# Attention into two MLPs on one core: two head pairs go over to split multiplication, and two weight units are prepared later

## The chip, the cores and the metric

The kernel runs on one core of a Trainium2 chip. The metric is the device time in microseconds (us) of one execution. The core has a matrix engine (TensorE, PE in the profile; its weight loads are PEld), a vector engine (VectorE, DVE), a scalar engine (ScalarE, ACT), GpSimd (POOL), and SyncE (SP), which issues this kernel's DMAs.

## The reference

```python
# q, k, v: 4 batches, 12 heads, 448 tokens, head size 64
scores = cap * tanh((q @ k.T / 8) / cap)
attn   = exp(scores - max(scores)); attn = attn / (sum(attn) + 1e-9)
x = (attn @ v)            # put together as 1792 tokens x 768
x = relu(x @ w_in)**2  @ w_out      # first MLP,  768 -> 2048 -> 768
x = relu(x @ w_in2)**2 @ w_out2     # second MLP, 768 -> 2048 -> 768
```

The weights arrive as 64-bit floats; all else is float32.

## The kernel before, in words

**Stages.** Attention works on pairs of heads, six pairs to a batch. Attention of batch 0 stands first. Then the first MLP is run batch by batch (generator `mlp(b, ...)`): batch 0 of it is woven with attention of batch 1, batch 1 with attention of batch 2, batch 2 with attention of batch 3. The last batch of the first MLP has no attention beside it, but `x2_side`, which puts together the second MLP's input. The second MLP (`mlp2`) takes the batches two by two, in halves h = 0 and h = 1; each half has two parts of 28 weight pieces.

**A multiplication in three terms.** The MLPs split each float32 operand into a high and a low part of the type fp32r (a copy on ScalarE, line 218 for weights, and a subtraction on VectorE, line 219), and multiply low by high, high by low and high by high: line 242 in the first MLP, 410 and 488 in the second.

**Native and split pairs.** After tanh and exp (lines 594 and 629) a pair multiplies its exponentials with v (line 642), over four chunks of keys; the fourth chunk is half as wide. A pair named in `NATIVE[b]` gives float32 exponentials to the matrix engine as they are, with a column of ones in v that makes the sum over keys. Any other pair is split: each chunk gets a high copy on ScalarE (`ph`, line 636) and a low part on VectorE (`pl`, line 637), VectorE adds the chunks up (`over_keys`, lines 602 to 607), GpSimd adds over the partitions (`over_partitions`, line 611, two instructions), and v is split once (lines 567 and 568). In `att_pair`:

```python
            if native:
                moving = [t[c]]
            else:
                ...
                ACT.activation(ph, t[c], AF.Copy)
                DVE.tensor_tensor(pl, t[c], f32(ph), op=ALU.subtract)
                over_keys(ALU.add, s, c)
                moving = [pl, ph]
```

**Weight units.** The second MLP uses weights that were recombined into blocks (seven products where eight would be needed). `prep_units` makes these in 16 units: unit u holds two raw pieces of 128 x 768 64-bit numbers. A unit loads both (line 176), decodes each (`dec`: one ScalarE and three VectorE instructions, lines 192 to 195), forms three differences and one sum on VectorE (lines 331 to 334), and stores seven blocks of 128 x 384 to DRAM (line 340). Units 0 to 7 belong to part 0, and unit n is used from block 7n of it; units 8 to 15 belong to part 1. `UNITS` has four lists: units prepared beside the first MLP's batches 1, 2 and 3, and beside the first third of the second MLP.

**What sets the order.** `weave` advances the side generators by the share of the main one's matmuls that was issued. A list of n units has 4n + 1 steps, spread evenly over 0.96 of a batch of the first MLP (576 matmuls), and over 0.34 of the second MLP's first half (1008 matmuls). Attention starts a pair every 7 steps (`LAG`). From there the tile framework plans each engine's queue at build time, and each queue runs in order. Instructions of the units are put behind the latest weight instruction of their engine (`behind`). Weights are split two pieces (of 18 matmuls) ahead of use (`S_AHEAD`).

Of the kernel before, what the change touches and what calls it, by code (L numbers as in the profile page):

```python
# [27 lines left out]
CAP_MAX = 32.0  # L28
L_AHEAD, D_AHEAD, S_AHEAD = 3, 2, 2
LAG0, LAG = 5, 7  # L30
NATIVE = ((0, 1, 2, 3, 4, 5), (0, 1, 4, 5), (1, 4), (1, 4))
T_BUFS, PH_BUFS, SPLIT_BUFS, RAW_BUFS, U_BUFS = 6, 2, 4, 2, 4
W_END = 0.96
G_ACT = (0, 2, 3)
E_FROM, E_STEP = 0, 3
UNITS = ((0, 1, 2), (3, 8, 9, 10), (11, 12, 13, 14, 15), (4, 5, 6, 7))
NS = 28
LINE = 128
RIGHT_PAD = 24
# [64 lines left out]
def program(ctx: ExitStack, tc, work, capv, sct, eps, qT, kT, v, v1, vl, w_in, w_out, out, guard):  # L104
# [3 lines left out]
    def pools(es, name, spec, **kw):  # L108
        return [es.enter_context(tc.tile_pool(name=f"{name}{i}_{guard}", bufs=n, **kw)) for i, n in enumerate(spec)]
# [191 lines left out]
    def prep_units(us):  # L301

        def load(u):
            part, n = divmod(u, 8)
            src = (w_in, w_out)[part][1]
            return [raw_load(src[n + 8 * j]) for j in range(2)]

        with behind():  # L310
            raws2 = load(us[0])
        for at, u in enumerate(us):
            yield
            part, n = divmod(u, 8)
            wa = []
            for j in range(2):
                with behind():
                    wa.append(prep["wa"].tile([P, CC, P], F32, tag="wa", name="wa"))
                    dec(raws2[j], wa[j])
                yield  # L320
            a = [[wa[j].rearrange("p c n -> p (c n)")[:, i * H3:(i + 1) * H3] for i in range(2)] for j in range(2)]
            if part == 0:
                (a11, a12), (a21, a22) = a
            else:
                (a11, a21), (a12, a22) = a
            with behind():
                if at + 1 < len(us):
                    raws2 = load(us[at + 1])
                ss = prep["ss"].tile([P, 3, H3], F32, tag="ss", name="ss")
                s1, (s2, s3, s4) = a21, (ss[:, i] for i in range(3))  # L330
                DVE.tensor_tensor(s3, a11, a21, op=ALU.subtract)
                DVE.tensor_tensor(s1, a21, a22, op=ALU.add)
                DVE.tensor_tensor(s2, s1, a11, op=ALU.subtract)
                DVE.tensor_tensor(s4, a12, s2, op=ALU.subtract)
            yield
            blocks = {"A11": a11, "A12": a12, "A22": a22, "S1": s1, "S2": s2, "S3": s3, "S4": s4}
            with behind():
                for i, name in enumerate(ORDER[part]):
                    k = n * 7 + i if part == 0 else i * 8 + n
                    nc.sync.dma_start(out=scr2[part][k // 2][:, (k % 2) * H3:(k % 2 + 1) * H3], in_=blocks[name])  # L340
# [187 lines left out]
    def is_native(b, pr):  # L528
        return pr in NATIVE[b]

# [203 lines left out]
    for b in range(B):  # L734
# [3 lines left out]
        else:  # L738
            us = UNITS[b - 1]
            if b < 3:  # L740
# [24 lines left out]
    prep.update(zip(("raw", "r", "wa", "ss"), pools(l1, "prep2_", (RAW_BUFS, 1, 2, 1), reuse_waits="tile")))  # L765
    us = UNITS[3]
    late_units = prep_units(us)
# [64 lines left out]
```

## Time and profile before

| | us |
|---|---|
| median of three runs (lowest, highest) | 1120.07 (1116.61, 1121.51) |
| the profiled execution | 1113.1 |
| its span, first to last instruction | 1111.3 |
| PE busy in the span | 1081.6 (97%) |
| DVE busy in the span | 863.0 (78%) |
| ACT busy in the span | 742.6 (67%) |
| mean granted share of TensorE's clock | 0.994 |

The busy time of an engine is the union of its instructions' times; matmuls overlap each other in the records, so that a matmul's own duration is longer than the step from one to the next. Idle time of an engine that is not the bound costs nothing.

### The profile page before, as it was taken

The page shows a single profiled execution, that of the slowest core. Times are in us where ns is not written, and L with a number is a line of the kernel's source. Part 1 is how long each engine was busy: PE and PEld are TensorE (multiplying, and loading weights), DVE is VectorE, ACT ScalarE, POOL GpSimd, SP SyncE. Part 2 cuts the span into 40 slices and gives each one's busy share as a digit, 9 for nine tenths or more (in the row PEclk, how much of TensorE's full clock was granted, in tenths as well). Part 3 has the DMA queues.
Part 4 walks back from the last instruction along what each step waited for, and adds up shares of the span by engine and source line. Part 5 has one row for each costly group of instructions (what it writes and reads, how often), then busy time and mean ns, then how long its engine had stood idle before and what let it go on. Part 6 is the DMA issues. An engine that isn't in the chain of part 4 may idle for free.

```text
span 1111.3 us, 14519 instructions
## 1 busy us (share of the span) xinstructions
PE 1081.6 (97%) x5088; PEld 948.1 (85%) x5088; DVE 863.0 (78%) x1146; ACT 742.6 (67%) x1038; POOL 63.5 (6%) x24
## 2 busy tenths in 40 slices
PE   6979989999999999999999999999999999999998
PEld 4446978889898799899899999999998999999997
DVE  7777999846989778899778876798688856566763
ACT  7998998538696759998747743555666525555542
POOL 0000220000222021022020000000000000000000
PEclk9998999999999999999999999999999999999999
DMA  8895668865746575755467886885335443333341
GB/s 333 296 293 195 194 222 274 284 205 158 240 140 209 163 258 184 238 188 204 147 229 257 303 293 226 278 320 163 108 120 177 141 150 112 114 100 114 130 134 67
DMA packets 92177, 221.11 MB, mean 199 GB/s; under 512 B 16576, under 2 KB 43072, under 8 KB 92096
## 3 DMA queue, kind: packets, MB, share of 16 engines
q1 hardware_dynamic: 92096, 220.10, 59.2%
q8 instruction: 42, 0.69, 0.2%
q14 instruction: 39, 0.32, 0.1%
HBM read 174.28 MB, written 45.70 MB: 198 GB/s over the span
## 4 chain that ended last, share of the span: by engine, by line
PE 83%; ACT 7%; DVE 4%; DMA 3%; issue 2%; SPq 0%; DVEq 0%; ACTq 0%
PE ps L242 36%; PE st L410 18%; PE st L488 16%; PE pv L642 8%; PE sc L589 5%; ACT t L594 1%; ACT t L629 1%; DMA raw<-w_in 1%; ACT whi L218 1%; ACT wf L192 1%; DVE wlo L219 1%; DMA work<-y 1%; ACT ph L636 0%; DMA comp<-work 0%; ACT work L655 0%
## 5 line engine op out<-in xcount | busy, mean ns | idle before, releaser
L219 DVE TENSOR_TENSOR wlo<-wf,whi 128x768 fp32r<-128x768 f32 x240 | 236.8, 988 | 67.8 <-ACT whi L218 66.8
L218 ACT ACTIVATE whi<-wf 128x768 fp32r<-128x768 f32 x240 | 201.4, 839 | 107.9 <-PE st L410 48.5
L242 PE MATMUL ps<-x,whi 128*128 128x448 f32 x768 | 219.7, 367 | 3.5 <-DVE x L690 3.5
L242 PE MATMUL ps<-g,whi 128*128 128x448 f32 x768 | 219.4, 366 | 0.0
L410 PE MATMUL st<-xx,whi 128*128 128x448 f32 x672 | 189.8, 365 | 0.0
L488 PE MATMUL st<-t,whi 128*128 128x448 f32 x672 | 185.4, 365 | 0.0
L242 PEld LDWEIGHTS ps<-x,whi 128*128 128x128 f32 x768 | 145.1, 189 | 17.5 <-DVE x L690 3.9
L242 PEld LDWEIGHTS ps<-g,whi 128*128 128x128 f32 x768 | 144.3, 188 | 14.0 <-issue 2.5
L242 PE MATMUL ps<-x,wlo 128*128 128x448 f32 x384 | 143.8, 377 | 1.5 <-ACT x L689 1.5
L242 PE MATMUL ps<-g,wlo 128*128 128x448 f32 x384 | 143.3, 375 | 0.0
L488 PEld LDWEIGHTS st<-t,whi 128*128 128x128 f32 x672 | 126.2, 188 | 9.9
L410 PEld LDWEIGHTS st<-xx,whi 128*128 128x128 f32 x672 | 126.2, 188 | 9.9
L410 PE MATMUL st<-xx,wlo 128*128 128x448 f32 x336 | 121.7, 365 | 0.0
L488 PE MATMUL st<-t,wlo 128*128 128x448 f32 x336 | 117.1, 365 | 0.7 <-ACT xx L343 0.7
L589 PE MATMUL sc<-ql,kk 128*128 128x448 f32 x192 | 79.1, 412 | 16.7 <-DVE kk L553 8.1
L594 ACT ACTIVATE t<-sc,sct 128x896 f32<-128x896 f32 x96 | 85.5, 914 | 12.4 <-PE sc L589 11.9
L611 POOL PARTITION_ALL_REDUCE work<-work x20 | 63.3, 3212 | 500.4 <-DVE work L605 383.3
L629 ACT ACTIVATE t<-t,capv 128x896 f32<-128x896 f32 x96 | 89.0, 952 | 0.3
L343 ACT ACTIVATE t<-g 128x896 fp32r<-128x896 f32 x48 | 45.4, 950 | 63.6 <-PE st L488 62.9
L242 PEld LDWEIGHTS ps<-x,wlo 128*128 128x128 f32 x384 | 72.5, 189 | 10.2 <-ACT x L689 1.8
L242 PEld LDWEIGHTS ps<-g,wlo 128*128 128x128 f32 x384 | 72.1, 188 | 8.3 <-issue 2.3
L344 DVE TENSOR_TENSOR t<-g,t 128x896 fp32r<-128x896 f32 x48 | 52.0, 1088 | 34.5 <-ACT t L343 34.1
(102 smaller groups left out, 1505.4 us busy)
## 6 DMA issues: line engine op xcount, KB each, us to landing
wf<-scr SPq DMA_DIRECT2D x215, 384.0 KB, 3.2
raw<-w_in SPq DMA_DIRECT2D x32, 768.0 KB, 6.1
raw<-w_out SPq DMA_DIRECT2D x32, 768.0 KB, 6.0
scr<-wf SPq DMA_DIRECT2D x32, 384.0 KB, 5.8
scr<-wa SPq DMA_DIRECT2D x64, 192.0 KB, 4.3
scr<-ss SPq DMA_DIRECT2D x48, 192.0 KB, 4.1
k_r<-kT SPq DMA_DIRECT2D x18, 448.0 KB, 4.1
q_r<-qT SPq DMA_DIRECT2D x18, 448.0 KB, 4.5
```

Source lines behind the costliest of these rows:

```text
L218: mark(ACT.activation(hi, f, AF.Copy))
L219: mark(DVE.tensor_tensor(lo, f, f32(hi), op=ALU.subtract))
L242: PE.matmul(ps, lhsT=w[:, i, :], rhs=x[part][:, j, :], start=first and n == 0, stop=last and n == len(terms) - 1)
L343: ACT.activation(hi, t, AF.Copy)
L344: DVE.tensor_tensor(lo, t, f32(hi), op=ALU.subtract)
L410: PE.matmul(ps, lhsT=w[:, i + c, :], rhs=x[:, kk_, c, :], start=first and c == 0 and n == 0, stop=c == 2 and n == 2, skip_group_check=not ...
L488: PE.matmul(banks[b][e], lhsT=w[:, 3 * f + e, :], rhs=x[:, f, :], start=first and q == f == n == 0, stop=q == 3 and f == 1 and n == 2, ski ...
L589: PE.matmul(sc[:, 0 if shared else j, :S], lhsT=kchunk(kk, j, c), rhs=q[:, j, :], start=n == 0 if shared else n % 2 == 0, stop=n == 3 if s ...
L594: ACT.activation(t[c], sc[:, 0, :S] if shared else sc[:, :, :S], AF.Tanh, scale=sct)
L611: POOL.partition_all_reduce(out[:, j], s[:, j], P, op)
L629: ACT.activation(t[c], t[c], AF.Exp, scale=capv)
L642: PE.matmul(pvs[j], lhsT=vv[:, j, c, :], rhs=m_ if c == KC else m_[:, j, :], start=c == 0 and m_ is moving[0], stop=c == KC and m_ is movi ...
```

## The change: one pair each of batches 2 and 3 is split, and the units are dealt out anew

```diff
-NATIVE = ((0, 1, 2, 3, 4, 5), (0, 1, 4, 5), (1, 4), (1, 4))
+NATIVE = ((0, 1, 2, 3, 4, 5), (0, 1, 4, 5), (4,), (4,))
...
-UNITS = ((0, 1, 2), (3, 8, 9, 10), (11, 12, 13, 14, 15), (4, 5, 6, 7))
+UNITS = ((0, 1), (8, 9, 10), (2, 11, 12, 13, 14, 15), (3, 4, 5, 6, 7))
```

Pair 1 of batch 2 and pair 1 of batch 3 are no longer native. The four lists of units go from 3, 4, 5 and 4 units to 2, 3, 6 and 5.

## Rows read from the trace of the kernel before

**Rows 1.** Busy time by stretch; columns: stretch, length, engines, clock, DMA share, GB/s.

```profile
core 0: us, PE busy (x) PEld busy (x) DVE busy (x) ACT busy (x) POOL busy (x), PEclk, DMA share, GB/s
254.10:417.40 163.30, 161.55 (x770) 142.42 (x769) 137.87 (x182) 121.60 (x178) 25.01 (x8) 1.00 0.60 194
...
417.40:579.80 162.40, 162.40 (x770) 142.65 (x769) 134.79 (x174) 129.75 (x195) 24.72 (x8) 1.00 0.58 194
...
579.80:696.50 116.70, 116.70 (x578) 108.17 (x577) 90.46 (x131) 70.79 (x114) 0.00 (x0) 1.00 0.78 269
```

**Rows 2.** The chain that ended last: start, length, what, how many.

```profile
91.89 6.01 PE pv L642 x16
...
357.59 2.85 DVE pl L637
360.48 1.89 PE pv L642 x8
...
396.02 1.62 PE pv L642 x8
...
568.92 127.68 PE ps L242 x630
```

**Rows 3.** Matrix engine's waits from 254 to 1106 us: total, times, longest.

```profile
PE pv L642 <- DVE pl L637: 1.7, 1, 1.7
PE st L488 <- ACT xx L343: 0.7, 1, 0.7
```

**Rows 4.** Groups by line of what a pair runs: busy, mean ns, idle before.

```profile
L642 PE MATMUL pv<-t,vv 128*65 128x448 f32 x128 | 52.7, 539 | 0.0
...
L636 ACT ACTIVATE ph<-t 128x896 fp32r<-128x896 f32 (+1 forms) x40 | 33.9, 862 | 1.6 <-PE pv L642 1.4
...
L605 DVE TENSOR_TENSOR work<-work,t 64x448 f32<-64x448 f32 x20 | 12.3, 616 | 0.3
...
L602 DVE TENSOR_TENSOR work<-t 128x896 f32<-128x896 f32 x10 | 10.9, 1085 | 5.3 <-ACT t L629 5.3
...
L568 DVE TENSOR_TENSOR vv<-v_r,vv 128x256 fp32r<-128x256 f32 x20 | 7.6, 414 | 0.2
...
L567 ACT ACTIVATE vv<-v_r 128x256 fp32r<-128x256 f32 x20 | 7.1, 402 | 0.0
```

**Rows 5.** The low parts and weight subtractions by source line: ns min/median/max.

```profile
L637 DVE TENSOR_TENSOR pl<-t,ph x40: 610/1084/2841, 116.7 to 565.4; 128x896 fp32r<-128x896 f32 x30, 128x448 fp32r<-128x448 f32 x10
...
L219 DVE TENSOR_TENSOR wlo<-wf,whi x240: 898/952/2798, 69.5 to 1093.5; 128x768 fp32r<-128x768 f32 x120
```

**Rows 6.** VectorE and GpSimd in order of time, about 489 us: start, length, what.

```profile
489.47 2.73 DVE L637 TENSOR_TENSOR pl<-t,ph 128x896 fp32r<-128x896 f32 x1
492.13 2.80 DVE L219 TENSOR_TENSOR wlo<-wf,whi 128x768 fp32r<-128x768 f32 x1
...
488.88 6.15 POOL L611 PARTITION_ALL_REDUCE work<-work  x2 [43.09 <-DVE work L605]
```

**Rows 7.** Groups by line of what a unit runs.

```profile
L194 DVE SCALAR_TENSOR_TENSOR r<-raw,r 128x768 int32<-128x768 int32 x64 | 62.8, 982 | 1.2
...
L193 DVE TENSOR_SCALAR r<-raw 128x768 int32<-128x768 uint32 x64 | 38.8, 606 | 6.2 <-DMA raw<-w_in 3.6 <-DMA raw<-w_out 2.0
...
L195 DVE SCALAR_TENSOR_TENSOR wa<-wa,r 128x768 int32<-128x768 int32 x32 | 32.3, 1010 | 1.0 <-ACT wa L192 0.4
...
L192 ACT ACTIVATE wa<-raw 128x768 f32<-128x768 f32 x32 | 28.8, 905 | 6.2 <-DMA raw<-w_in 4.3 <-DMA scr<-wa 2.0
...
L332 DVE TENSOR_TENSOR wa<-wa 128x384 f32<-128x384 f32 x16 | 10.4, 653 | 0.1
...
L334 DVE TENSOR_TENSOR ss<-wa,ss 128x384 f32<-128x384 f32 x16 | 8.8, 552 | 0.2
```

**Rows 8.** Busy time by stretch inside batches 1 and 2 of the first MLP.

```profile
264.00:294.00 30.00, 30.00 (x150) 27.80 (x149) 29.84 (x40) 26.25 (x41) 6.00 (x2) 1.00 0.57 192
294.00:324.00 30.00, 30.00 (x136) 24.43 (x135) 25.38 (x40) 24.73 (x38) 0.00 (x0) 1.00 0.50 160
324.00:364.00 40.00, 38.25 (x189) 35.12 (x188) 39.71 (x49) 29.88 (x44) 12.55 (x4) 1.00 0.62 202
...
428.00:508.00 80.00, 80.00 (x380) 70.06 (x379) 72.41 (x96) 74.96 (x119) 12.48 (x4) 1.00 0.60 198
```

**Rows 9.** Busy time in the second MLP, while units are prepared, and behind that.

```profile
704.00:768.00 64.00, 64.00 (x318) 59.32 (x317) 57.97 (x85) 41.55 (x48) 0.00 (x0) 1.00 0.79 272
768.00:793.60 25.60, 25.60 (x128) 23.73 (x127) 19.91 (x26) 14.37 (x17) 0.00 (x0) 1.00 0.39 124
```

## The prediction, made before the changed kernel ran

> **What bounds the kernel now.** I read the busy time by stretch first. In batches 1 and 2 of the first MLP, where the change takes pairs, the matrix engine is busy 161.55 of 163.30 us and 162.40 of 162.40; in the last batch, which gets a unit, 116.70 of 116.70, at full granted clock [rows 1]. Its list of waits says the same: from 254 us on it waits 1.7 us once for the low part of an attention chunk, and 0.7 us in the second MLP [rows 3]. So these stretches last as long as their matmuls. The reader should check that against the chain: 630 matmuls of the last batch stand in it as 127.68 us without a break, 0.2027 us from one to the next [rows 2]. VectorE is next, with 84% and 83% of the two attention stretches, and ScalarE has 74% and 80% [rows 1]. The change takes work from the engine that is the bound and adds some to the two behind it. The question is how full these are just where it lands.
>
> **What a split pair saves the matrix engine.** Eight native pairs outside batch 0 have 128 records of the multiplication with v, so 16 to a pair [rows 4]. Their mean of 539 ns overlaps the next record's, so I take the step: in the chain 16 of them last 6.01 us, one pair. Eight of a split pair last 1.62 us [rows 2]; it has four chunks by two heads by two terms, 16 matmuls, 3.24 us. The saving is 2.77 us a pair, 5.54 us for two, all of it on the path as long as the matrix engine stays the bound.
>
> **What a split pair adds elsewhere.** VectorE: three full low parts by 1.084 us and a half one by 0.610 [rows 5], 3.86 us; sums over the keys, two full ones by 1.085 (the second like the first) and two halves by 0.616, 3.40 us; two splits of v by 0.414, 0.83 us [rows 4]. That is 8.09 us. ScalarE: four high copies by 0.862 and two of v by 0.402, 4.25 us [rows 4]. The closing instructions of the two kinds of pair are two and two on either engine; I count their difference as nothing.
>
> GpSimd gets two all-reduces, and these cost VectorE something that no row of its own tells. While they run at 488.88 for 6.15 us, a low part takes 2.73 us and a weight subtraction 2.80 [rows 6], against medians of 1.084 and 0.952 [rows 5]: 1.65 and 1.85 us more, 3.5 us a pair. So a split pair costs VectorE 8.09 + 3.5 = 11.6 us.
>
> The Trainium skill (GPSIMD Engine Reference, Key points) says that GpSimd shares its SBUF interfaces with VectorE and that instructions with two SBUF inputs contend; both held instructions have two, so the trace agrees. The page has no price. If VectorE stood still for the whole 6.15 us, a pair would cost 14.2 us; if contention were nothing, 8.09; the sum goes by the 3.5 us of the rows.
>
> **What a unit takes along.** VectorE: two decodes of 0.606 + 0.982 + 1.010 us and then 0.653 and three of about 0.552, 7.5 us; ScalarE two by 0.905, 1.8 us [rows 7]. DMA: by the code two loads of 128 x 768 x 8 bytes and seven stores of 128 x 384 x 4, 2.95 MB.
>
> **Batches 1 and 2.** Each loses one unit and gains one split pair: VectorE +4.1 us, ScalarE +2.4, matrix engine -2.77. VectorE then has 142.0 of 160.5 us (88%) and 138.9 of 159.6 (87%). On the average it fits. But the load isn't even. In batch 1, VectorE has 29.84 of 30 us from 264 to 294 and 39.71 of 40 from 324 to 364; what room there is (4.6 us) lies between, at pair 1, because pair 1 is native [rows 8]. The change fills just that room with 11.6 us. Against it stands the unit work that has gone by 358 us: before, two units (15.0 us); after, with 9 steps spread over the batch instead of 13, one unit and one or two decodes (10.1 to 12.7). Relief is 2.3 to 4.9 us, so 6.7 to 9.3 us meet the 5.07 us that VectorE is idle from 264 to 364 us (100 less 29.84, 25.38 and 39.71), and the matrix engine is there 2.77 us earlier. VectorE falls behind by another 4.4 to 7.0 us at the place where the one wait stands today: the low part of pair 3's third chunk, itself held 2.85 us, ends and its matmuls start at once [rows 2].
>
> How much of this lag ends on the matrix engine, the trace doesn't show. From below: nothing, and today's 1.7 us goes as well, if other matmuls are queued ahead; weights are split two pieces ahead, 36 matmuls or 7.3 us. From above: the whole 7.0 us. The nearest rows are near the lower end: 39.71 of 40 us of VectorE cost 1.75 us of matrix engine, and in batch 2, with pairs 2 and 3 split, 72.41 of 80 us of VectorE and 74.96 of 80 of ScalarE cost nothing [rows 3, 8]. I take 1.5 us more in batch 1, and 0.5 us in batch 2 (bounds 0 and 4.4), where VectorE has more room and ScalarE, at 94%, gets 2.4 us. Batch 1: -2.77 + 1.5 = -1.3 us. Batch 2: -2.77 + 0.5 = -2.3 us.
>
> **The last batch.** A sixth unit brings VectorE to 98.0 of 116.7 us and ScalarE to 72.6; the DMA share of 0.78, at 269 GB/s some 31.4 MB [rows 1], rises to 0.85. Nothing there ends on the path: 0, at most 1 us if a weight load lands late. Unit 2 goes first there and is used from the second MLP's 127th matmul on, a whole batch later.
>
> **The second MLP.** A fifth unit in the same third. VectorE is busy 57.97 of 64 us [rows 9]; with 7.5 more it needs 65.5 of 64. It ends 1.5 us late, and behind that 5.7 of 25.6 us are free [rows 9]. The weights' 7.3 us cover that; if the cover fails for an instant, what is late next are the weight subtractions. I take 0.5 us, with bounds of 0 and 3.75 (half a unit standing ahead of a weight). Unit 3 is new here and is used earliest: its blocks from the 190th matmul on, 38 us into the half. Its stores are planned at 0.065 of the half, 13 us in, so no wait is counted.
>
> **The sum** is -1.3 - 2.3 + 0 + 0.5 = -3.0 us (rounded). The profiled execution took 1113.1 us (span 1111.3 and 1.8 around it) and would take 1110.1. It lies 7 us under the median of the three runs, and the saving is the same on both: 1120.07 - 3.0 = **1117.0 us**.
>
> **Rivals.** *The full saving.* VectorE's lag stays off the path, and the present 1.75 us goes too: -7.3 to -5.6 us, about 1113.5. For it: batch 2 has full engines and no wait. Against it: in batch 1 the lag grows where a wait stands already.
>
> *VectorE becomes the bound* from 264 to 364 us (slower). The lag of 4.4 to 7.0 us goes wholly to pair 3's low parts: batch 1 alone ends 1.6 to 4.2 us later than before, and batch 2 saves little; in all +1 to +6, about 1123. It decides as soon as more than 5.5 us of new waits arise. For it: the 39.71 of 40 us, and that the new all-reduces hold VectorE. Against it: the units spread thinner there.
>
> *The second MLP's first third overflows.* Five units at 7.5 us beside 57.97 of 64 us; weights come late one after the other, up to 3.75 us, and the total is -2 to +1, about 1120. For it: a VectorE over 100% on paper. Against it: nothing else is late there today.
>
> **How the numbers follow.** Forecast (-5.5 to -0.5) 0.50; full saving 0.20; VectorE as bound 0.18; overflow 0.12. A measurement of this kernel can't tell less than about 0.5%, 5.6 us, from no change. The full saving is faster by that: 0.20. Slower by that are two thirds of the VectorE case, where lags in both batches add up, and a little of the overflow: 0.13. The rest, 0.67, is the same. The range takes in the full saving and half the unknown of the lag, and 1 to 2 us for the spread of the three runs (1116.61 to 1121.51): 1111.5 to 1124.5. The bounds of all terms together would give -7.3 to +11.
>
> **What would show it.** Right: the two attention stretches each shorter by 1 to 3 us; ten split pairs become twelve, with 24 all-reduces; the matrix engine's waits for low parts between 2 and 5 us in batch 1, none in the last batch, under 1 us from 700 to 770 us. Wrong: waits of the matrix engine for weights in the second MLP, for unit blocks from DRAM, or a stretch of batch 1 as long as 163.3 us or longer. The prediction fails if the planner's new queue order moves matmuls of attention to other places than before, since all slacks here are read from the old order.

## The result, and the profile after

The changed kernel takes 1125.83 us (median of 7 runs, 1118.49 to 1128.14) against 1116.16 (7 runs, 1113.75 to 1121.51). The ratio of the runs is 1.0061, 95% interval 1.0039 to 1.0084 (the quotient of the two medians alone would be 1.0087): slower by about 6.8 us. The prediction was 3.0 us faster, in a range up to 1124.5; it started from a median of three runs, 1120.07, which lies 3.9 us above that of the seven. The profiled execution has a span of 1121.3 us, 10.0 more than before, and 24 all-reduces instead of 20.

Busy time by stretch of the changed kernel, with the columns of [rows 1]: batches 1, 2 and 3 of the first MLP and the two halves of the second. A stretch goes from its first matmul to that of the next.

```profile
core 0: us, PE busy (x) PEld busy (x) DVE busy (x) ACT busy (x) POOL busy (x), PEclk, DMA share, GB/s
...
255.56:421.10 165.54, 160.37 (x769) 142.80 (x768) 140.84 (x182) 123.94 (x182) 32.32 (x10) 1.00 0.52 172
421.10:586.78 165.68, 160.43 (x770) 142.83 (x768) 139.38 (x174) 132.32 (x197) 32.88 (x10) 1.00 0.55 180
586.78:704.79 118.01, 116.99 (x577) 108.12 (x576) 94.66 (x138) 70.95 (x114) 0.00 (x0) 1.00 0.82 280
704.79:911.33 206.54, 205.68 (x1010) 189.02 (x1009) 173.69 (x232) 121.30 (x151) 0.00 (x0) 1.00 0.60 199
911.33:1115.78 204.45, 204.45 (x1009) 189.16 (x1007) 126.95 (x152) 101.09 (x119) 0.00 (x0) 1.00 0.35 113
```

The same five stretches took 163.28, 162.36, 116.73, 205.19 and 204.45 us before (the first three within 0.04 us of [rows 1]). So batch 1 is 2.3 us longer, batch 2 3.3, batch 3 1.3, the first half of the second MLP 1.35, the last half as long. The two halves before:

```profile
696.43:901.62 205.19, 204.53 (x1009) 189.27 (x1008) 168.15 (x222) 119.51 (x149) 0.00 (x0) 1.00 0.55 186
901.62:1106.07 204.45, 204.45 (x1009) 189.16 (x1007) 126.93 (x152) 101.09 (x119) 0.00 (x0) 1.00 0.35 113
```

Another 1.5 us stand ahead of batch 1, where no pair and no unit was changed; over all profiles of this study that point lies between 254.06 and 257.33 us, so this is scatter.

The reader should subtract: length less PE busy is the time in which the matrix engine had nothing to run. It was 1.75 us in batch 1 and nothing in batch 2 [rows 1, 8]; now it is 5.17 and 5.25. Batch 1's own matmuls need 163.28 - 1.75 - 2.77 = 158.8 us and batch 2's 162.36 - 2.77 = 159.6, so the stretches are 6.8 and 6.1 us longer than that; 5.2 us of each is that idle time, the rest isn't told apart here.

What the matrix engine waits for, from 255 us to the end (total, times, longest), beside [rows 3]:

```profile
PE pv L642 <- DVE pl L637: 5.3, 5, 2.1
PE pv L642 <- DVE u L661: 4.0, 3, 2.6
PE ps L242 <- ACT relu L262: 1.0, 1, 1.0
PE sc L589 <- DVE ql L554: 1.0, 2, 0.7
PE st L410 <- DVE wlo L219: 0.7, 1, 0.7
```

The low parts were foreseen as the place, though at pair 3. The first long wait of batch 1 stands at the new pair itself: its own all-reduces run from 306.69 us, two instructions of VectorE beside them take 2.60 and 2.37 us (0.95 and 0.62 otherwise), and the low part of its third chunk comes behind these:

```profile
306.69 6.33 POOL L611 PARTITION_ALL_REDUCE work<-work  x2 [20.71 <-DMA raw<-w_in]
...
307.22 2.60 DVE L219 TENSOR_TENSOR wlo<-wf,whi 128x768 fp32r<-128x768 f32 x1
309.74 0.55 DVE L331 TENSOR_TENSOR ss<-wa 128x384 f32<-128x384 f32 x1
310.21 2.37 DVE L267 TENSOR_TENSOR relu<-relu 128x448 f32<-128x448 f32 x1
...
314.44 1.08 DVE L637 TENSOR_TENSOR pl<-t,ph 128x896 fp32r<-128x896 f32 x1
...
315.57 0.48 PE L642 MATMUL pv<-pl,vv 128*128 128x448 f32 x1 [2.07 <-DVE pl L637]
```

Line 661 was not foreseen: it is the closing instruction that reads a pair's result out of PSUM, and the next pair's first multiplication with v waits until that bank is free. The longest such wait, in order of time (GpSimd, then VectorE, then the matrix engine):

```profile
356.78 6.82 POOL L611 PARTITION_ALL_REDUCE work<-work  x2 [18.65 <-DMA q_r<-qT]
...
357.31 3.47 DVE L219 TENSOR_TENSOR wlo<-wf,whi 128x768 fp32r<-128x768 f32 x2
360.70 2.31 DVE L193 TENSOR_SCALAR r<-raw 128x768 int32<-128x768 uint32 x1
363.04 0.63 DVE L661 TENSOR_TENSOR u<-pv,rest 64x448 f32<-64x448 f32 x1
...
363.81 0.44 PE L642 MATMUL pv<-pl,vv 128*128 128x448 f32 x1 [2.61 <-DVE u L661]
```

While two all-reduces run, VectorE gets two weight subtractions and one step of a decode done, 5.8 us for what takes 1.9 and 0.6 us otherwise [rows 5, 7]; the closing instruction stands behind them in its queue, and the matrix engine stands still for 2.61 us. These two all-reduces are pair 3's. The kernel before ran them too, from 354.01 us, and its one wait of 1.75 us stood beside them.

### The profile page after: what moved, and what is told of

Same layout as the page of the kernel before. It is cut to its first block, busy times and chain, and to the rows that moved or that the text cites. A ratio compares the mean times of both kernels' runs of the same rounds, so it can differ in the third digit from the quotient of the medians.

```text
span 1121.3 us, 14563 instructions
## 1 busy us (share of the span) xinstructions
PE 1081.2 (96%) x5088; PEld 949.1 (85%) x5088; DVE 881.3 (79%) x1166; ACT 750.1 (67%) x1050; POOL 78.9 (7%) x28
## 4 chain that ended last, share of the span: by engine, by line
PE 59%; DVE 18%; DMA 10%; ACT 9%; issue 4%; SPq 0%; DVEq 0%; ACTq 0%
PE ps L242 23%; PE st L488 16%; PE st L410 11%; PE pv L642 6%; DVE wlo L219 4%; PE sc L589 3%; DMA scr<-wa 2%; DMA raw<-w_in 2%; DVE pl L637 2%; ACT t L594 2%; DVE g L268 1%; ACT whi L218 1%; DVE r L194 1%; ACT t L629 1%; DMA wf<-scr 1%
## 5 line engine op out<-in xcount | busy, mean ns | idle before, releaser
L611 POOL PARTITION_ALL_REDUCE work<-work x24 | 78.7, 3329 | 491.8 <-DVE work L605 452.5
```

The source lines that it names most:

```text
L611: POOL.partition_all_reduce(out[:, j], s[:, j], P, op)
```

## The experiments

**Pairs or units?** The first four kernels take the change apart.

```diff
 pairs_only:  NATIVE as changed, UNITS as before
 units_only:  UNITS as changed, NATIVE as before
 pair_b2:     UNITS as changed, NATIVE = (..., (4,), (1, 4))
 pair_b3:     UNITS as changed, NATIVE = (..., (1, 4), (4,))
```

> Pair 1 of batches 2 and 3 is split, the unit lists stay as before. VectorE theory (the 11.6 us that a split pair brings to VectorE, with the two all-reduces' hold in it, end as waits of the matrix engine in the two attention stretches): with no unit gone from there, VectorE gets 7.5 us more in each than in the changed kernel, so slower than it: +8 to +15 us against the kernel before; the last batch and the second MLP as long as before. Unit theory (the cost is the sixth unit in the last batch and the fifth in the second MLP): faster than before by 2 to 6 us. Planner theory (any edit reorders the queues, and the new order costs): no rule, between -5 and +10.

> Only the unit lists change, all pairs stay native as before. VectorE theory: the attention stretches lose 7.5 us of VectorE each and the one wait of 1.7 us goes; the last batch and the second MLP lengthen by no more than the 2.6 us that the changed kernel's profile shows there: -2 to +1 us against before. Unit theory: the whole loss is here, +5 to +9 us. Planner theory: anything from -3 to +8.

> The changed kernel with pair 1 of batch 3 native again: pair 1 of batch 2 alone is split, units as in the changed kernel. VectorE theory: the stretch with batch 2's attention keeps its +2.3 us of the changed kernel's profile, the stretch with batch 3's has its old matmuls and less unit work, so it is as long as before; with up to 2.6 us from the late units +2 to +5 us. Unit theory: +2.6 less one pair's saving of 2.8, about 0. If the two pairs' costs add, this and the run with the other pair alone differ from the unit lists alone by as much as the changed kernel does in all.

> The changed kernel with pair 1 of batch 2 native again: pair 1 of batch 3 alone is split. VectorE theory: the stretch with batch 3's attention keeps its +3.3 us, the other loses its wait of 1.7 us; with up to 2.6 us from the late units +2 to +5 us. Unit theory: about 0.

| kernel | ratio to before | interval | idle PE: batch 1, batch 2 (us) |
|---|---|---|---|
| changed | 1.0061 | 1.0039 to 1.0084 | 5.17, 5.25 |
| pairs only | 1.0075 | 1.0048 to 1.0102 | 5.54, 6.33 |
| units only | 1.0013 | 0.9992 to 1.0035 | 0.00, 0.86 |
| pair of batch 2 alone | 1.0044 | 1.0020 to 1.0069 | 3.43, 0.47 |
| pair of batch 3 alone | 1.0041 | 1.0018 to 1.0063 | 0.00, 5.50 |

Batches 1 and 2 with the units alone, by stretch:

```profile
255.01:416.25 161.24, 161.24 (x770) 142.64 (x769) 132.34 (x172) 120.06 (x176) 26.06 (x8) 1.00 0.55 175
416.25:579.27 163.02, 162.16 (x770) 142.31 (x769) 130.33 (x166) 129.03 (x193) 26.65 (x8) 1.00 0.57 185
```

With one pair split, the stretch with that pair, of batch 2 and of batch 3:

```profile
255.29:420.41 165.12, 161.69 (x769) 144.56 (x768) 140.35 (x181) 123.37 (x180) 32.31 (x10) 0.99 0.54 174
418.15:583.88 165.73, 160.23 (x769) 142.85 (x768) 139.35 (x174) 132.35 (x197) 32.88 (x10) 1.00 0.55 179
```

The pairs are most of the loss. Each costs about 0.3% above the units alone (1.0044 and 1.0041 against 1.0013; the intervals overlap), and each lengthens its own stretch: 165.12 us where the units alone have 161.24, and 165.73 where they have 163.02. The unit theory is out: it wanted +5 to +9 us from the units. They are not free, though: what they cost in the second MLP comes below. Taking a unit out of batch 1 does what was said: the stretch falls to 161.24 us without a wait.

**Which engine makes the new waits?** Five kernels, each the changed one but for the edit shown, `reduce_native` the one before.

```diff
 no_reduce:
-        if not native:
+        if not native and not (b > 1 and pr == 1):
             over_partitions(ReduceOp.add, s, sb)
 reduce_native (in the kernel before):
-        if not native:
+        if not native or (b > 1 and pr == 1):
             over_partitions(ReduceOp.add, s, sb)
 no_vector (no_reduce, and in pair 1 of b > 1):
-                DVE.tensor_tensor(pl, t[c], f32(ph), op=ALU.subtract)
-                over_keys(ALU.add, s, c)
-                moving = [pl, ph]
+                moving = [ph, ph]
 no_scalar (in pair 1 of b > 1):
-                ACT.activation(ph, t[c], AF.Copy)
-                DVE.tensor_tensor(pl, t[c], f32(ph), op=ALU.subtract)
+                DVE.tensor_tensor(pl, t[c], t[c], op=ALU.subtract)
...
-                moving = [pl, ph]
+                moving = [pl, pl]
 squares_act:
-G_ACT = (0, 2, 3)
+G_ACT = (0, 1, 2, 3)
```

> The changed kernel without GpSimd's two all-reduces in pair 1 of batches 2 and 3 (left out; these pairs divide by an older sum). All else of the split pair stays. If the all-reduces' hold of VectorE (3.5 us a pair) is what tips the stretches: both get 2 to 3.5 us shorter, +1 to +3 us against before. If it is VectorE's own added instructions (8.1 us a pair): shorter by under 1.5 us each, +4 to +7.

> The kernel before, with two all-reduces of GpSimd added to the native pair 1 of batches 2 and 3 (of sums that are already there; the result isn't used). It adds nothing to VectorE's instructions. If a hold costs the matrix engine what it costs VectorE: +3.5 us a pair, +5 to +7 in all. If there is room for it at pair 1 (4.6 us of idle VectorE from 294 to 324 us): 0 to +2.

> The changed kernel; in pair 1 of batches 2 and 3 VectorE's low parts and sums and GpSimd's all-reduces are left out, and the high copy is multiplied twice, so that the matrix engine and ScalarE do as much as in the changed kernel. VectorE theory: the matrix engine's saving shows in full, the two attention stretches take 158.8 to 160.5 us; with the late units' 1 to 2 us, -4 to -1 us against before. Theory of the planner's order or of ScalarE: waits of 2 us and more stay in both stretches, +2 to +6.

> The changed kernel without ScalarE's high copies in pair 1 of batches 2 and 3 (3.4 us a pair); VectorE subtracts as often as before, with t in the place of the high copy, and the result is multiplied twice. Sums and all-reduces stay. ScalarE as second bound: the waits in batch 2 of the first MLP fall from 5.25 us to under 2.5, those in batch 1 stay at 3 to 5; +2 to +5 us against before. VectorE with the hold as the only bound: no change in either stretch, +6 to +8.

> The changed kernel, and the first MLP's batch 1 squares the second operand on ScalarE as batches 0, 2 and 3 do: VectorE loses 16 squares of 0.614 us (9.8 us) in the stretch with batch 2's attention, ScalarE gains 16 of 0.578 (9.2 us). The matrix engine's work is the same, and so are pairs and units. VectorE theory: that stretch goes from 165.5 us to 159 to 161.5, the next one stays at 165.7; in all 4 to 6 us faster than the changed kernel, +1 to +3 us against before. Theory that the new wait is in the split pair's own chain (exp, high copy, low part, sums, all-reduce one after the other, however free VectorE is): the stretch stays at 164 to 166 us, or gets longer as ScalarE is fuller; +6 to +9 against before.

Ratios to before: no_reduce 1.0021 (1.0000 to 1.0042), reduce_native 1.0015 (0.9992 to 1.0039), no_vector 1.0049 (1.0019 to 1.0079), no_scalar 1.0041 (1.0019 to 1.0063), squares_act 1.0126 (1.0096 to 1.0155). Batches 1 and 2 of each, in this order (without all-reduces; native pair with them; without VectorE's work; without ScalarE's copies; squares on ScalarE):

```profile
255.74:416.53 160.79, 159.34 (x770) 143.23 (x768) 137.46 (x182) 124.64 (x182) 25.99 (x8) 1.00 0.55 178
416.53:580.29 163.76, 160.32 (x769) 142.86 (x768) 135.91 (x174) 132.20 (x197) 26.14 (x8) 1.00 0.57 182
```
```profile
257.12:423.21 166.09, 162.77 (x769) 142.02 (x768) 140.57 (x182) 121.61 (x178) 31.42 (x10) 1.00 0.60 190
423.21:587.46 164.25, 163.34 (x770) 142.22 (x769) 137.44 (x173) 128.50 (x193) 30.45 (x10) 1.00 0.59 191
```
```profile
256.23:418.46 162.23, 159.92 (x769) 143.26 (x768) 132.28 (x174) 123.85 (x182) 25.54 (x8) 1.00 0.56 175
418.46:584.44 165.98, 160.51 (x769) 142.94 (x768) 129.81 (x166) 132.17 (x197) 26.45 (x8) 1.00 0.56 179
```
```profile
255.04:423.11 168.07, 162.82 (x769) 144.16 (x768) 140.98 (x182) 120.69 (x178) 32.32 (x10) 0.99 0.53 170
423.11:585.46 162.35, 160.39 (x769) 142.89 (x768) 137.79 (x174) 129.28 (x193) 32.34 (x10) 1.00 0.56 184
```
```profile
256.97:421.15 164.18, 159.79 (x770) 143.12 (x768) 134.41 (x168) 131.58 (x199) 32.42 (x10) 1.00 0.53 164
421.15:593.04 171.89, 163.41 (x770) 144.00 (x768) 139.43 (x173) 131.79 (x196) 31.40 (x10) 0.99 0.57 184
```

The two stretches answer differently. In batch 1 the idle time falls from 5.17 us to 1.45 without the all-reduces and stays at 5.25 without ScalarE's copies: here the all-reduces' hold of VectorE is the cause. In batch 2 it falls to 1.96 without ScalarE's copies and stays at 5.47 without all of VectorE's work: here ScalarE's copies weigh most. My VectorE theory was wrong for batch 2, and by the whole amount. These readings rest on the idle time in the profiles; the ratios alone don't tell the kernels apart, and the run without all of VectorE's work (1.0049), which leaves out more than the one without all-reduces (1.0021), is not faster than it. The kernel with squares on ScalarE missed both its forecasts, at 14 us slower than before and with batch 1 at 164.18 us where the VectorE theory had 159 to 161.5: what VectorE got back in batch 1 (140.84 to 134.41 us) ScalarE took on (123.94 to 131.58), and the idle time stays at 4.39 us. Why its batch 2, whose code is the same, rose to 8.48 us wasn't tried. With all-reduces added to a native pair, where VectorE has room, the time doesn't move measurably, though batch 1 shows 3.32 us of waits instead of 1.75.

**Do these waits recur?** Three kernels were profiled a second time.

> The changed kernel once more, for a second profile. If the matrix engine's waits come from the kernel and its queue order, they are in the same places: 5.17 us in batch 1 of the first MLP and 5.25 us in batch 2, each within 1 us. If they are chance of one execution, they differ by 2 us and more.

> The run without VectorE's low parts and sums and without all-reduces in pair 1, once more, for a second profile. Load theory (ScalarE's high copies make the waits of batch 2): 2.3 us of waits in batch 1 and 5.5 us in batch 2, each within 1 us. Chance: they differ by 2 us and more.

> The run without the all-reduces of pair 1, once more, for a second profile. Load theory: 1.5 us of waits in batch 1 and 3.4 in batch 2, each within 1 us; the all-reduces then cost batch 1 3.7 us and batch 2 1.8. Chance: they differ by 2 us and more.

Idle time in batches 1 and 2, first and second profile: changed 5.17 and 5.25, then 4.12 and 4.92 (1128.48 us); without VectorE's work 2.31 and 5.47, then 2.76 and 4.23 (1125.83); without all-reduces 1.45 and 3.44, then 1.64 and 2.72 (1117.18). They recur, to 1.3 us (two of the six differ by more than the 1 us expected), and at the same places: 2.07 and 2.61 us in batch 1 of the changed kernel, then 1.91 and 2.20. The changed kernel's second profile:

```profile
256.38:422.50 166.12, 162.00 (x770) 145.92 (x768) 140.77 (x182) 124.08 (x182) 32.31 (x10) 0.98 0.52 172
422.50:588.57 166.07, 161.15 (x769) 142.87 (x768) 139.36 (x174) 132.48 (x197) 32.87 (x10) 1.00 0.56 179
```

What batch 2 gains without all-reduces, about 2 us, stays beside the 5 us without all of VectorE's work: the parts don't add, and that is left open. The wait in batch 3 (1.02, then none) doesn't recur. In the second MLP the size doesn't (0.86, then 0.31; without VectorE's work 2.87, then 0.38; without all-reduces 0.90, then 2.27), but the loss does. Its first half takes 205.96 to 209.49 us in all thirteen profiles with five units beside it, and 204.28 to 205.76 in the four with four: some 2 us more in the mean, with 1.4 us of idle time against 0.3. In eleven of the thirteen, and in none of the four, the matrix engine waits there for a weight's low part (line 410 for line 219), 0.2 to 2.4 us. So the fifth unit is a cost of its own.

**Was there a saving to be had?** Two kernels leave pair 1, of what the split adds, only its matmuls and the two splits of v; in the second the matmuls are twice as many.

```diff
 mm_only (from no_vector, in pair 1 of b > 1):
-            ACT.activation(t[c], t[c], AF.Exp, scale=capv)
...
-                ACT.activation(ph, t[c], AF.Copy)
+                ACT.activation(ph, t[c], AF.Exp, scale=capv)
                 moving = [ph, ph]
 mm_long:
-                moving = [ph, ph]
+                moving = [ph, ph, ph, ph]
```

> The changed kernel with nothing left of the split pair 1 (batches 2 and 3) but its 16 short matmuls and the two splits of v: exp writes the type fp32r directly, that is multiplied twice, and the high copies, low parts, sums and all-reduces are left out. Load theory (the waits come from what the pair adds to VectorE, GpSimd and, in batch 2 of the first MLP, ScalarE): ScalarE loses 3.4 us a pair and VectorE 7.3, so both stretches run at the matmuls' own 158.8 and 159.6 us with less than 1 us of waits, and with the late units -5 to -2 us against before. Order theory (the new queue order makes matmuls of attention wait for one another's banks and for closing instructions, whatever the load): 2 us and more of waits stay in the stretch of batch 2, -1 to +4.

> The run with the bare matmuls (high copies, low parts, sums and all-reduces of pair 1 left out in batches 2 and 3), but each high copy is multiplied four times, so that pair 1 costs the matrix engine 32 steps of 0.2025 us, 6.5 us, 0.5 more than as a native pair; the other engines do what they do there. Pace theory (VectorE and ScalarE set the pace at pairs 2 and 3, and a matrix engine that is there 2.77 us earlier just waits): the waits of 2.30 and 2.48 us in the two attention stretches go to 0 to 1 us, and the stretches take 161.5 to 163 us, hardly longer than with the short matmuls (161.50 and 163.73). Order theory (the queues' new order itself makes the waits): 2 us and more stay in each, and the stretches take 164 to 166 us.

Ratios: 1.0020 (0.9997 to 1.0042) and 0.9999 (0.9969 to 1.0028). Batches 1 and 2, first with 16 matmuls to a pair, then with 32:

```profile
256.38:417.88 161.50, 159.20 (x769) 143.22 (x768) 132.83 (x174) 120.96 (x178) 25.39 (x8) 1.00 0.56 177
417.88:581.61 163.73, 161.25 (x770) 144.53 (x768) 129.77 (x166) 129.39 (x193) 25.51 (x8) 0.99 0.57 183
```
```profile
255.77:417.74 161.97, 161.97 (x786) 146.32 (x784) 132.60 (x174) 120.76 (x178) 25.54 (x8) 1.00 0.55 176
417.74:581.63 163.89, 163.89 (x785) 146.39 (x784) 128.27 (x166) 129.59 (x193) 25.51 (x8) 1.00 0.56 180
```

What the matrix engine waits for in the two stretches with the short matmuls, and the 3.4 us behind the longest of these waits:

```profile
PE sc L589 <- DVE ql L554: 2.5, 1, 2.5
PE pv L650 <- DVE pl L645: 2.2, 2, 1.2
...
496.80:500.20 3.40, 3.39 (x10) 3.04 (x11) 3.30 (x5) 3.40 (x6) 0.00 (x0) 0.52 0.84 294
```

This is the plainest result of the study. With hardly any added work on the other engines, the short matmuls leave 2.30 and 2.48 us idle, of 2.77 saved. That the waits stay is what the order theory had forecast for this kernel; the load theory (under 1 us) missed. Give the matrix engine 3.24 us more a pair, and the stretches grow by 0.47 and 0.16 us; the idle time goes to 0.00. The units alone say the same: with native pairs, the same unit lists, and VectorE and ScalarE as busy to within 1 us, these stretches take 161.24 and 163.02 us, no more than with 2.77 us less of matmuls. The other engines set the pace behind pair 1, and the saving just turns into a wait for them. In batch 1 that is shown cleanly. In batch 2 the short kernel ran at half the clock for 3.4 us behind its one long wait, about 1.7 us lost by my estimate; without that its stretch would be some 162 us, and up to 1 us of the saving would have shown. The order theory foresaw 2 us and more of waits with the long matmuls too, and there it fails. Whether the other engines come late by their load or by the order of their queues, these kernels, each with a queue order of its own, don't tell.

**One unit moved, and no pair.** From the kernel before, with all pairs as they were:

```diff
-UNITS = ((0, 1, 2), (3, 8, 9, 10), (11, 12, 13, 14, 15), (4, 5, 6, 7))
+UNITS = ((0, 1), (3, 8, 9, 10), (2, 11, 12, 13, 14, 15), (4, 5, 6, 7))
```

> The kernel before; all pairs as before, and of the unit lists one change alone: unit 2 goes from batch 1 to the last batch of the first MLP, where six units cost 0 to 1 us in the profiles so far. The 1.75 us wait of batch 1 goes, batch 2 and the second MLP stay. Load theory: -2 to -1 us against before, a version that beats both. Order theory: -2 to +3, no rule.

The ratio is 0.9979 (0.9958 to 1.0001), 2.3 us faster than before, just short of certain; clearly faster than the changed kernel. Batches 1 to 3 and the two halves of the second MLP:

```profile
255.16:416.40 161.24, 161.24 (x770) 142.64 (x768) 132.30 (x172) 119.98 (x176) 26.07 (x8) 1.00 0.56 176
416.40:578.76 162.36, 162.36 (x770) 142.61 (x768) 135.06 (x174) 129.94 (x195) 24.72 (x8) 1.00 0.60 197
578.76:695.49 116.73, 116.73 (x577) 108.17 (x576) 96.49 (x141) 71.33 (x115) 0.00 (x0) 1.00 0.85 293
695.49:901.25 205.76, 205.38 (x1010) 189.21 (x1009) 167.89 (x222) 119.69 (x149) 0.00 (x0) 1.00 0.56 185
901.25:1109.72 208.47, 208.47 (x1009) 189.03 (x1007) 127.02 (x152) 101.19 (x119) 0.00 (x0) 1.00 0.35 111
```

Batch 1 is 2.0 us shorter, and the sixth unit costs batch 3 nothing. With four units still beside it, the first half of the second MLP keeps its length (205.76 us). The units alone differ from this kernel only in that unit 3 goes there too, and come out at 1.0013.

## Why the prediction was wrong, point by point

*"All of it on the path as long as the matrix engine stays the bound"* is the step that failed first. The saving of 2.77 us a pair was worked out rightly from the chain, but a matrix engine that is busy 98.9% or 100% of a stretch was taken for one with nothing close behind. The short and the long matmuls show that in these stretches 2.3 to 2.5 us of the saving come back as waits before anything else is added. So batch 1, forecast 1.3 us shorter, came out 2.3 us longer, and batch 2, forecast 2.3 us shorter, 3.3 us longer. The loads themselves came as worked out: VectorE is busy 140.84 and 139.38 us (142.0 and 138.9 forecast), ScalarE 123.94 and 132.32 (124.0 and 132.2 by the forecast's +2.4). What they cost the matrix engine did not.

*"I take 1.5 us more in batch 1, and 0.5 us in batch 2."* The rise of idle time was 3.4 and 5.25 us. For batch 1 the working gave a lag of 4.4 to 7.0 us with the right cause in it (the all-reduces' hold: 3.7 us of waits go with them, 2.5 by the second profiles), but at one place only, pair 3, where half of the waits stands, by the closing instruction; the other half stands at pair 1 itself. The error was to go by the lower bound because the nearest rows showed so little. Those rows were of a kernel that still had a native pair in front of pairs 2 and 3. For batch 2 the cause was missed: ScalarE at 94% was named, given 2.4 us and passed over. The run without VectorE's work (5.47 us) and the bare matmuls (2.48) differ in ScalarE's high copies, by 3.0 us, or 1.75 with the second profile of the former (4.23).

*Relief by the unit* was right: without the pairs, batch 1 is at 161.24 us, and with the unit left in (pairs only) the ratio rises to 1.0075, though the interval takes in the 1.0061.

*The last batch 0, the second MLP 0.5 us.* The first is right in size: the wait of 1.02 us doesn't recur. The second was too small: 1.35 us in this profile and some 2 us over all. It came by the way of the overflow rival, weights late in the first third, and by a sign that the prediction had named as wrong, "waits of the matrix engine for weights in the second MLP".

*The rivals.* "VectorE becomes the bound", with +1 to +6 us, is the nearest to what came (+6.8), right for batch 1 and with the wrong engine for batch 2. The other sign named as wrong, "a stretch of batch 1 as long as 163.3 us or longer", came with it: 165.54 us.

## What to carry to other kernels

That an engine is busy all of a stretch says that it has no idle time to lose, not that its time alone sets the length. Here VectorE stood at 99% over 40 us of batch 1, and VectorE and ScalarE at 91 and 94% over 80 us of batch 2 [rows 8], and less work for the matrix engine bought almost nothing. Test it the cheap way first: make the suspected work longer or shorter by itself, as with the 32 and 16 matmuls, before paying for the saving on the other engines. And when work is added at the only place where a busy engine has room, count the room as gone for what comes behind it.

## What the runs showed of the hardware

A wait can cost more than its length. In the second profile of the changed kernel the granted clock fell to half behind two waits of about 2 us. Three stretches around the first of them:

```profile
313.00:316.40 3.40, 1.49 (x8) 1.05 (x7) 3.40 (x7) 2.73 (x5) 0.45 (x1) 0.99 0.33 80
316.40:319.80 3.40, 3.40 (x11) 3.02 (x10) 3.40 (x7) 3.37 (x5) 0.00 (x0) 0.50 0.95 339
319.80:323.00 3.20, 3.20 (x18) 2.96 (x17) 3.20 (x7) 3.17 (x5) 0.00 (x0) 1.00 0.59 196
```

The matrix engine idles for 1.91 us in the first, and then runs at 1.2 GHz instead of 2.4 for 3.4 us: 11 matmuls touch that stretch, against 18 in the 3.2 us behind it. Half the clock for 3.4 us is, by my estimate, some 1.7 us lost. In the first profile it did not happen behind waits of 2.07 and 2.61 us at the same places, so this adds scatter to the changed kernel's time. Over all seventeen profiles, eight of the fourteen waits between 1.86 and 3.47 us in the two attention stretches have a stretch at half the clock behind them; a mean clock of 0.99 or 0.98 in the rows above is the mark of one or two.

The Trainium skill (TensorE: Matmul & The Clock Gate, Part 1) says that the clock goes to half when the engine has been idle; the rows agree that it does, but behind eight of fourteen like waits.

Matmuls can also be 2% slower at full granted clock: the last half of the second MLP took 204.45 us before and in the changed kernel, and 208.47 us in the kernel with one unit moved, with the same matmuls, no idle time and a clock of 1.00. Seven of the seventeen profiles show those 4 us, so two spans can differ by that much for nothing in the code. No run tells the cause.
